# Linear attention into a mixture of experts: the route's exponential and first rows moved, sixteen key projections as two column tiles, loads and fills in smaller pieces

## The chip, the cores and the metric

The kernel runs on one core of one Trainium2 chip. The metric is device time in microseconds; 427.6 us is the median of three runs of the kernel before (426.96 to 427.92). A smaller number is better.

## What is computed

Linear attention over 4 batches, 8 heads, 576 positions and head width 64, whose output rows (2304 tokens of 512) go through a mixture of 8 experts with one expert per token and a capacity of 576 rows per expert:

```python
def phi(x):
    proj = np.einsum('bhsd,df->bhsf', x, w_phi)
    proj = proj - np.max(np.abs(proj), axis=-1, keepdims=True)
    return np.concatenate([np.exp(proj), np.exp(-proj)], axis=-1)
q_p, k_p = (phi(q), phi(k))
kv = np.einsum('bhsf,bhsd->bhfd', k_p, v)
z = np.sum(k_p, axis=2)
num = np.einsum('bhsf,bhfd->bhsd', q_p, kv)
den = np.einsum('bhsf,bhf->bhs', q_p, z)[..., None] + 1e-06
x = num / den                                  # one row of 512 per token
...
logits = x @ w_gate
expert_idx = np.argmax(logits, axis=1)         # and its softmax weight
h = np.maximum(np.einsum('ecd,edf->ecf', disp, w1), 0.0)
y = np.einsum('ecf,efd->ecd', h, w2)
out[i] = gate_w[i] * y[expert_idx[i], pos[i]]  # rows beyond capacity stay zero
```

## The kernel before

The tokens are worked in two passes `p` of 1152 rows (nine blocks `r` of 128), the heads in two groups `g` of four. Each pass has 18 key items and then 18 query items, 72 in all; the loop in `attention` goes over steps `t`, and an item's stages run at lags behind the step in which its projection is made. Items 0 to 17 are the first pass's keys, 18 to 35 its queries, 36 to 53 the second pass's keys, 54 to 71 its queries. All engines' instructions are issued in the order in which this loop writes them, so each engine's queue is an order by hand.

A key item is: `project` (lines 246 to 261), which multiplies a block of `stk` by the two halves `whi` and `wlo` of `w_phi` into `pr` in PSUM (two buffers); `center` (lines 263 to 272) on VectorE, the maximum `m` and the difference `d` (three buffers), each followed by `tick`; `k_exp` on ScalarE, two exponentials `kp` (lines 315 and 316); and four steps later `kv_sum` (line 342), the product of `kp` and the values into `acc`, written as two 64-wide halves. A query item is: projection, `d`, four transposes `pt` (line 356), two exponentials `qp`, and `q_num` (line 371), also in 64-wide halves; then `rows_out` divides.

`stk` is made from a loaded block `px` by ScalarE (line 194, a copy to f16) and GpSimd (line 195, the remainder); `x_split` issues both. The table `plan` gives the steps of each split and, eight steps ahead of it, of its load (`x_load`, line 186), on SP's queue. `beat[0]` is the last `d`; a load that is `paced` waits for it. The gate's share of the values is worked by `vgate` in units of four blocks (lines 219, 229 and 241), in the first pass at steps 2, 5, 9, 13 and 16 and the next two.

`route` works out, for a group of blocks (9, then 4, 3 and 2), which expert each token goes to and at what row of `xs`. It is a list of small steps; `tick` and the loop let one or two of them run at a time, between the attention's own VectorE operations. `sm_t` is one PSUM bank in which the small results lie. For the first group the list also finds the expert with most tokens: `swaps` (a matmul of totals, three VectorE steps, then `swap_all`, nine small GpSimd operations), which swaps the experts' places. `perm["s"]` (written as `perms` in the trace) is each expert's first row. `exps` (line 481) is the exponential `es` of the logits on ScalarE; `sums` reduces it.

```python
            *([number, exps] if late else [exps] if old is None else []),
            lambda: v.tensor_reduce(rn[:, 0], oh.rearrange("p n e -> p e n"), AX.X, ALU.add),
            run_total,
            *([*swaps(), rest, rest, rest] if old is None else []),
            lambda: v.tensor_tensor(sel, oh, perm["s"].unsqueeze(1).to_broadcast([P, n, NE]), ALU.mult),
```

Then `scatter` (line 459) writes rows to `xs` from GpSimd's queue, from step 56 on. Before that `xs` is filled with zeros by `fill_xs` from SP. After attention the experts run one after the other: `ffn1` (lines 814 to 817), `relu`, `ffn2` (lines 845 to 848) and a scatter to `out`.

## Time and profile before

| | |
|---|---|
| median of three runs | 427.6 us (426.96 to 427.92) |
| the profiled execution | 425.98 us, of which its span 424.2 us |
| PE busy | 405.1 us, 95% of the span |
| PEld (weight loads) busy | 357.7 us, 84% |
| VectorE (DVE) busy | 265.9 us, 63% |
| ScalarE (ACT) busy | 245.9 us, 58% |
| GpSimd (POOL) busy | 175.4 us, 41% |
| mean granted TensorE clock | 0.99 |

Times in rows are from the span's start. A busy share is a mean over stages with different limits, so the rows further down are taken stage by stage: which engine waits, and for what. "[2.33 <-DVE d L269]" behind an instruction says that its engine was idle for 2.33 us before it and that the instruction at line 269 released it. A matmul's record is longer than its step, since matmuls are pipelined; the distance of two starts is the step. An f32 matmul shows as two records.

### The profile page before, as it was taken

To read this page: it belongs to the slowest core of one execution; us is meant where nothing else is said; L and a number is where in the kernel's file an instruction comes from. 1 tells how busy PE (TensorE), PEld (TensorE's weight loads), DVE (VectorE), ACT (ScalarE), POOL (GpSimd) and SP (SyncE) were. 2 spreads that over 40 slices of the span, in tenths; PEclk is the share of its full clock that TensorE was granted. 3 is DMA by queue.
4 is the path that set the end of the run, shared out by engine and by line. 5 is a ranking of instruction groups with operands and counts; after the bars stand their busy time and mean duration, and the time that the engine had idled before them with its cause. 6 is when DMAs were issued, how large, how long until landed. Compare 5 with 4: busy or idle time off the path is not lost.

```text
span 424.2 us, 12166 instructions
## 1 busy us (share of the span) xinstructions
PE 405.1 (95%) x4813; PEld 357.7 (84%) x4813; DVE 265.9 (63%) x585; ACT 245.9 (58%) x452; POOL 175.4 (41%) x215
## 2 busy tenths in 40 slices
PE   6999999999799989999999999999999999999992
PEld 4788888888789878989979898989898998799871
DVE  5776898887788797833247975757475464156410
ACT  3978687779776766712146855656565454155410
POOL 1848566448576778730035306042241500160011
PEclk9999999999899999999999999999999999999997
DMA  7990599489506743479007995977959176210010
GB/s 254 388 353 5 170 328 372 138 287 307 172 6 222 227 171 107 175 249 368 5 32 223 341 338 192 331 226 224 324 179 349 64 240 228 93 36 0 2 51 29
DMA packets 42715, 82.78 MB, mean 195 GB/s; under 512 B 4351, under 2 KB 9343, under 8 KB 42624
## 3 DMA queue, kind: packets, MB, share of 16 engines
q1 hardware_dynamic: 38080, 72.13, 50.5%
q0 software_dynamic: 4544, 9.47, 6.2%
q8 instruction: 53, 0.87, 0.9%
q14 instruction: 38, 0.31, 0.2%
HBM read 62.65 MB, written 24.30 MB: 205 GB/s over the span
## 4 chain that ended last, share of the span: by engine, by line
PE 83%; POOL 4%; issue 4%; ACT 4%; DVE 3%; DMA 1%; POOLq 0%; ACTq 0%
PE ph L814 9%; PE ph L815 9%; PE ph L817 9%; PE acc L342 8%; PE acc L371 5%; PE sm L847 4%; PE sm L845 4%; PE sm L848 4%; PE ph L845 4%; PE ph L847 4%; PE ph L848 4%; PE pr L259 3%; PE pr L260 2%; PE pr L254 2%; PE pt L747 2%
## 5 line engine op out<-in xcount | busy, mean ns | idle before, releaser
L169 POOL DMA_INDIRECT out<-y,it x22 | 24.4, 1111 | 164.4 <-ACT y L860 86.7
L123 DVE TENSOR_TENSOR l<-raw,h 128x512 fp32r<-128x512 f32 x118 | 79.6, 706 | 19.6 <-ACT h L117 16.9
L195 POOL TENSOR_TENSOR stk<-px,stk 64x1024 f16<-64x1024 f32 (+1 forms) x30 | 70.8, 2363 | 38.6 <-ACT stk L194 37.7
L814 PE MATMUL ph<-xh,h 128*128 128x256 f32 (+3 forms) x292 | 79.4, 298 | 0.1
L815 PE MATMUL ph<-xh,l 128*128 128x256 f32 (+3 forms) x292 | 78.9, 296 | 0.0
L117 ACT ACTIVATE h<-raw 128x512 fp32r<-128x512 f32 x128 | 75.7, 629 | 0.0
L828 ACT ACTIVATE h<-ph 128x256 fp32r<-128x256 f32 (+3 forms) x67 | 28.8, 429 | 53.6 <-PE ph L817 52.9
L831 DVE SCALAR_TENSOR_TENSOR h<-ph,h 128x256 fp32r<-128x256 f32 (+2 forms) x91 | 33.3, 388 | 39.2 <-ACT h L828 38.8
L814 PEld LDWEIGHTS ph<-xh,h 128*128 128x128 f32 x292 | 55.6, 191 | 1.2 <-issue 0.2
L815 PEld LDWEIGHTS ph<-xh,l 128*128 128x128 f32 x292 | 55.7, 191 | 0.9
L265 DVE TENSOR_REDUCE m<-pr 128x4 f32<-128x512 f32 x72 | 49.2, 684 | 8.6 <-PE pr L260 5.1
L269 DVE TENSOR_TENSOR d<-pr,m 128x512 f32<-128x512 f32 x72 | 49.7, 691 | 4.0 <-ACT kp L316 0.4
L817 PE MATMUL ph<-xh,h 128*128 128x256 f32 (+3 forms) x292 | 50.9, 296 | 0.0
L342 PE MATMUL acc<-v,kp 128*64 128x73 f32 (+1 forms) x1280 | 46.3, 231 | 1.1 <-issue 1.1
L342 PEld LDWEIGHTS acc<-v,kp 128*64 128x64 f32 (+1 forms) x1280 | 40.7, 138 | 5.8 <-issue 2.6
L371 PE MATMUL acc<-kv,qp 128*64 128x73 f32 x1152 | 44.5, 229 | 0.0
L371 PEld LDWEIGHTS acc<-kv,qp 128*64 128x64 f32 x1152 | 39.1, 136 | 6.0 <-issue 5.7
L817 PEld LDWEIGHTS ph<-xh,h 128*128 128x128 f32 x292 | 42.7, 191 | 0.6
L259 PE MATMUL pr<-whi,stk 128*128 128x128 f16 x260 | 36.9, 223 | 2.6 <-DVE d L269 2.3
L260 PE MATMUL pr<-wlo,stk 128*128 128x128 f16 x260 | 36.4, 221 | 0.0
L194 ACT ACTIVATE stk<-px 64x1024 f16<-64x1024 f32 (+1 forms) x30 | 34.5, 1150 | 0.5
L358 ACT ACTIVATE qp<-pt 128x512 f32<-128x512 f32 x36 | 21.5, 596 | 21.1 <-PE pt L356 21.0
(163 smaller groups left out, 715.8 us busy)
## 6 DMA issues: line engine op xcount, KB each, us to landing
raw<-in_w SPq DMA_DIRECT2D x28, 1024.0 KB, 7.9
xs<-fill SPq DMA_DIRECT2D x18, 514.0 KB, 6.1
xr<-xs SPq DMA_DIRECT2D x24, 257.0 KB, 7.9
raw<-in_w SPq DMA_DIRECT2D x8, 512.0 KB, 4.3
vt<-in_vT SPq DMA_DIRECT2D x3, 1152.0 KB, 12.7
v<-in_vv SPq DMA_DIRECT2D x2, 1314.0 KB, 11.9
px<-in_kT SPq DMA_DIRECT2D x5, 512.0 KB, 8.5
px<-in_qT SPq DMA_DIRECT2D x4, 640.0 KB, 9.3
```

Of the source, the lines that this page charges most:

```text
L117: nc.scalar.activation(hi, a, AF.Copy)
L123: engine.tensor_tensor(lo, a, hi.bitcast(F32), ALU.subtract)
L195: return lambda: nc.gpsimd.tensor_tensor(t[other], x, t[own], ALU.subtract)
L259: nc.tensor.matmul(pr[:, j], lt, whi, start=True, stop=False)
L260: nc.tensor.matmul(pr[:, j], lt, wlo, start=False, stop=True)
L265: nc.vector.tensor_reduce(m.rearrange("p a b -> p (a b)"), pr, AX.X, ALU.max, apply_absolute_value=True)
L269: beat[0] = nc.vector.tensor_tensor(d, pr, m.to_broadcast([P, 4, NF]), ALU.subtract)
L342: nc.tensor.matmul(acc[f:f + D, a, j * GC:(j + 1) * GC], kp[lo:hi, j, a, f:f + D], vt[lo:hi, r, h * GC:(h + 1) * GC], start=first and j == ...
L371: nc.tensor.matmul(num[lo:hi, g, j * GC:(j + 1) * GC], qp[:, a, j, lo:hi], kv_t[b][:, a, 4 * g + j], start=(a == 0), stop=(a == 1))
L814: nc.tensor.matmul(acc, hi[:, k, fs], xh[:, k, o:o2], start=(k == 0), stop=False)
L815: nc.tensor.matmul(acc, lo[:, k, fs], xh[:, k, o:o2], start=False, stop=False)
L817: nc.tensor.matmul(acc, hi[:, k, fs], xl[:, k, o:o2], start=False, stop=(k == 3))
```

## The change

Five things are changed. `exps` of the first group goes behind `swaps`. A copy puts `perm["s"]` into the PSUM bank, and `sel` reads it there. Sixteen key projections (all of the first pass that use `stk`, eleven, and the second pass's first five) are written as two 64-wide halves for each of `whi` and `wlo`. The loads of keys and queries come in halves, a step apart, paced by the beat, seven steps ahead of the split (four for the first pass's queries); the second pass's values come in twelve pieces in place of four. The fills are 36 of 128 rows from step 19 to 53, where they were 18 of 256 rows from step 18 to 47.

```diff
--- before.py
+++ after.py
@@ -150,14 +150,8 @@
         tc.add_manual_dep(dma.ins, beat[0].ins.name, mybir.DependencyInfo(
             mybir.DependencyClass.Sync, mybir.DependencyReason.DATA), reason="pace")
 
-    def fill_xs(i, n):
-        r0, r1 = (NE * slots * j // n for j in (i, i + 1))
-        nr = (r1 - r0) // P
-        if nr:
-            paced(nc.sync.dma_start(xs[r0:r0 + nr * P, :].rearrange("(r p) c -> p r c", p=P),
-                                    fill.unsqueeze(1).to_broadcast([P, nr, XW])))
-        if r1 - r0 - nr * P:
-            nc.sync.dma_start(xs[r0 + nr * P:r1, :], fill[0:r1 - r0 - nr * P])
+    def fill_xs(r0, r1):
+        paced(nc.sync.dma_start(xs[r0:r1, :], fill[0:r1 - r0]))
 
     tokf = cpool.tile([P, NT // P], F32, tag="tokf", name="tokf")
     nc.gpsimd.iota(tokf, pattern=[[P, NT // P]], base=SKIP, channel_multiplier=1,
@@ -183,7 +177,9 @@
             raw_x[kind, p, g, c] = px_p.tile([P, 2, c1 - c0], F32, tag=f"px{c}", name="px")
         lo, hi = (0, cut) if cut > 0 else (-cut, c1 - c0)
         src = (kT if kind == "k" else qT)[2 * g:2 * g + 2, :, p * TP + c0 + lo:p * TP + c0 + hi]
-        nc.sync.dma_start(raw_x[kind, p, g, c][:, :, lo:hi], src.rearrange("i d c -> d i c"))
+        dma = nc.sync.dma_start(raw_x[kind, p, g, c][:, :, lo:hi], src.rearrange("i d c -> d i c"))
+        if beat[0] is not None:
+            paced(dma)
 
 
     def x_split(kind, p, g, c, odd):
@@ -256,8 +252,14 @@
         else:
             for j in range(4):
                 lt = stk[kind, p, g, c, j % 2][:, j // 2, cols]
-                nc.tensor.matmul(pr[:, j], lt, whi, start=True, stop=False)
-                nc.tensor.matmul(pr[:, j], lt, wlo, start=False, stop=True)
+                if kind == "q" or p and (g or r >= 5):
+                    nc.tensor.matmul(pr[:, j], lt, whi, start=True, stop=False)
+                    nc.tensor.matmul(pr[:, j], lt, wlo, start=False, stop=True)
+                    continue
+                for w in (whi, wlo):
+                    for o in range(0, P, D):
+                        nc.tensor.matmul(pr[o:o + D, j], lt[:, o:o + D], w, start=w is whi, stop=w is wlo,
+                                         skip_group_check=True)
         return pr
 
     def center(pr):
@@ -532,11 +534,12 @@
             lambda: v.scalar_tensor_tensor(ef, lt, 0.0, io, ALU.is_ge, ALU.mult),
             lambda: v.tensor_reduce(flat(ix), ef, AX.X, ALU.min),
             lambda: v.tensor_tensor(oh, ix.to_broadcast([P, n, NE]), io, ALU.is_equal),
-            *([number, exps] if late else [exps] if old is None else []),
+            *([number, exps] if late else []),
             lambda: v.tensor_reduce(rn[:, 0], oh.rearrange("p n e -> p e n"), AX.X, ALU.add),
             run_total,
-            *([*swaps(), rest, rest, rest] if old is None else []),
-            lambda: v.tensor_tensor(sel, oh, perm["s"].unsqueeze(1).to_broadcast([P, n, NE]), ALU.mult),
+            *([*swaps(), exps, rest, rest, rest, lambda: v.tensor_copy(sm_t[:, TOT:TOT + NE], perm["s"])]
+              if old is None else []),
+            lambda: v.tensor_tensor(sel, oh, sm_t[:, TOT:TOT + NE].unsqueeze(1).to_broadcast([P, n, NE]), ALU.mult),
             lambda: v.tensor_reduce(flat(sl), sel, AX.X, ALU.add),
             positions,
             *([] if late or old is None else [exps, rest, rest, rest]),
@@ -630,7 +633,9 @@
                 ends.append(max(split))
                 if x[:2] != (K, 0):
                     free = ends[-4] if len(ends) > 3 else 6
-                    load_at.setdefault(max(free + 2, min(split) - 8), []).append((*x, c))
+                    first = max(free + 2, min(split) - (4 if x[:2] == (Q, 0) else 7))
+                    for i in range(2):
+                        load_at.setdefault(first + i, []).append((*x, c, (1 - 2 * i) * (runs[c][1] - runs[c][0]) // 2))
 
         plan(0, [(5, 6), (12, 13), (15, 16), (25, 26), (31, 32), (42, 44), (46, 49)])
         plan(1, [(3, 4), (10, 11), (19, 21), (23, 24), (28, 29), (37, 39), (55, 51), (57, 53)])
@@ -662,7 +667,8 @@
             for i, f in enumerate(parts):
                 early.setdefault(t + min(i, 3 - t) if t == 2 else t + i, []).append(f)
 
-        FILLS = [*range(18, 36, 3), *range(36, 48)]
+        FILLS = [*range(19, 36, 2), *range(36, 54), *range(37, 54, 2)]
+        filled = [0]
         OPEN = 56
         depth = 4
         for t in range(len(items) + depth):
@@ -684,15 +690,13 @@
                 for _ in range(4):
                     if pending:
                         step()
-            if t in FILLS:
-                for i in range(len(FILLS)):
-                    if FILLS[i] == t:
-                        fill_xs(i, len(FILLS))
-            if t in (19, 23):
-                vt_load(1, 0, NBLK, (t - 19) // 4)
-                v_load(1, 0, NBLK, (t - 19) // 4)
+            for _ in range(FILLS.count(t)):
+                fill_xs(filled[0], min(filled[0] + P, NE * slots))
+                filled[0] += P
+            if 19 <= t < 31:
+                (vt_load if t % 2 else v_load)(1, (t - 19) // 2 % 3 * 3, (t - 19) // 2 % 3 * 3 + 3, (t - 19) // 6)
             if t == 54:
-                assert swapped
+                assert swapped and filled[0] >= NE * slots
                 for e in range(NE):
                     who[e] = nc.values_load(perm_i[0:1, e:e + 1], engines=[mybir.EngineType.SP], min_val=0,
                                             max_val=NE - 1)
```

ScalarE's order in the second pass's key phase. `kp` are a key item's exponentials, `stk` the copy of a split, `es` the route's exponential. Before:

```order
L194 ACTIVATE stk<-px 64x1280
L315 ACTIVATE kp<-d 128x4x128
L316 ACTIVATE kp<-d 128x4x128
L481 ACTIVATE es<-sm 128x72
L315 ACTIVATE kp<-d 128x4x128
L316 ACTIVATE kp<-d 128x4x128
L315 ACTIVATE kp<-d 128x4x128
L316 ACTIVATE kp<-d 128x4x128
```

Now, from the next item on:

```order
L317 ACTIVATE kp<-d 128x4x128
L318 ACTIVATE kp<-d 128x4x128
L317 ACTIVATE kp<-d 128x4x128
L318 ACTIVATE kp<-d 128x4x128
L190 ACTIVATE stk<-px 64x1280
L317 ACTIVATE kp<-d 128x4x128
L318 ACTIVATE kp<-d 128x4x128
L317 ACTIVATE kp<-d 128x4x128
L318 ACTIVATE kp<-d 128x4x128
L483 ACTIVATE es<-sm 128x72
```

`es` stood one item behind the first `stk` half; now it stands four items further down, behind the second half too.

VectorE's order in the same phase. `m` and `d` are an item's maximum and difference, `sm<-oh` the sum of the one-hot rows at old line 536 (now 538), `rb` its cast, `swap<-sm` the first step of `swaps`. Before:

```order
L269 TENSOR_TENSOR d<-pr,m 128x512
L265 TENSOR_REDUCE m<-pr 128x4
L536 TENSOR_REDUCE sm<-oh 128x8
L269 TENSOR_TENSOR d<-pr,m 128x512
L265 TENSOR_REDUCE m<-pr 128x4
L476 CAST rb<-sm 128x8
L269 TENSOR_TENSOR d<-pr,m 128x512
L265 TENSOR_REDUCE m<-pr 128x4
L269 TENSOR_TENSOR d<-pr,m 128x512
L350 COPY kv<-acc 128x2x292
L265 TENSOR_REDUCE m<-pr 128x4
L503 TENSOR_REDUCE swap<-sm 128x1
```

Now:

```order
L271 TENSOR_TENSOR d<-pr,m 128x512
L267 TENSOR_REDUCE m<-pr 128x4
L538 TENSOR_REDUCE sm<-oh 128x8
L478 CAST rb<-sm 128x8
L271 TENSOR_TENSOR d<-pr,m 128x512
L267 TENSOR_REDUCE m<-pr 128x4
L271 TENSOR_TENSOR d<-pr,m 128x512
L267 TENSOR_REDUCE m<-pr 128x4
L505 TENSOR_REDUCE swap<-sm 128x1
L271 TENSOR_TENSOR d<-pr,m 128x512
```

`rb` and the first step of `swaps` each come up by one item.

VectorE's order at the end of that phase, where `sel` is made. Before:

```order
L269 TENSOR_TENSOR d<-pr,m 128x512
L265 TENSOR_REDUCE m<-pr 128x4
L539 TENSOR_TENSOR sel<-oh,perms 128x72
L269 TENSOR_TENSOR d<-pr,m 128x512
L540 TENSOR_REDUCE sm<-sel 128x9
```

Now:

```order
L271 TENSOR_TENSOR d<-pr,m 128x512
L540 COPY sm<-perms 128x8
L267 TENSOR_REDUCE m<-pr 128x4
L542 TENSOR_TENSOR sel<-oh,sm 128x72
L271 TENSOR_TENSOR d<-pr,m 128x512
L543 TENSOR_REDUCE sm<-sel 128x9
```

The copy `sm<-perms` stands ahead of the last item's `m`, and `sel` reads `sm` in place of `perms`.

## Rows read from the trace of the kernel before

**Rows 1.** The page: PE busy in tenths, 40 slices; the chain that ended last.

```profile
PE   6999999999799989999999999999999999999992
...
PE 83%; POOL 4%; issue 4%; ACT 4%; DVE 3%; DMA 1%; POOLq 0%; ACTq 0%
```

**Rows 2.** Stretches: length; busy PE, PEld, DVE, ACT, POOL; granted clock, DMA share, GB/s.

```profile
106.00:108.40 2.40, 0.07 (x4) 0.01 (x1) 0.94 (x3) 1.43 (x4) 2.05 (x1) 1.00 1.02 377
108.40:111.70 3.30, 3.30 (x43) 2.96 (x44) 2.63 (x6) 3.04 (x5) 0.56 (x1) 0.50 0.86 279
```

**Rows 3.** Timeline of PE: start, us, engine line operation, count [idle before <-releaser].

```profile
104.82 1.25 PE L342 MATMUL acc<-v,kp 128*64 128x73 f32 x32
108.40 0.29 PE L259 MATMUL pr<-whi,stk 128*128 128x128 f16 x1 [2.33 <-DVE d L269]
...
109.36 2.21 PE L342 MATMUL acc<-v,kp 128*64 128x73 f32 x32
...
112.18 1.25 PE L342 MATMUL acc<-v,kp 128*64 128x73 f32 x32
```

**Rows 4.** Timeline of VectorE (DVE), the reduction at line 536.

```profile
107.46 0.29 DVE L536 TENSOR_REDUCE sm<-oh 128x8 f32<-128x72 bf16 x1 [3.50 <-ACT es L481]
```

**Rows 5.** Timeline of ScalarE (ACT), 103 to 109 us.

```profile
103.46 0.61 ACT L316 ACTIVATE kp<-d 128x512 f32<-128x512 f32 x1
...
105.03 1.25 ACT L194 ACTIVATE stk<-px 64x1280 f16<-64x1280 f32 x1
...
107.22 0.21 ACT L481 ACTIVATE es<-sm 128x72 f32<-128x72 f32 x1
108.45 0.63 ACT L315 ACTIVATE kp<-d 128x512 f32<-128x512 f32 x1 [1.02 <-DVE d L269]
```

**Rows 6.** Timeline of VectorE, the products named sel.

```profile
125.27 0.17 DVE L546 TENSOR_TENSOR sel<-sm,oh 128x72 f32<-128x72 f32 x1
...
149.50 3.04 DVE L539 TENSOR_TENSOR sel<-oh,perms 128x32 f32<-128x32 bf16 x1
```

**Rows 7.** Timeline of GpSimd (POOL) at the same times.

```profile
123.45 2.13 POOL L195 TENSOR_TENSOR stk<-px,stk 64x1024 f16<-64x1024 f32 x1 [1.02 <-ACT stk L194]
...
149.98 2.49 POOL L123 TENSOR_TENSOR l<-raw,h 128x512 fp32r<-128x512 f32 x2
```

**Rows 8.** Timeline of PE in the second pass's query phase.

```profile
147.64 1.24 PE L371 MATMUL acc<-kv,qp 128*64 128x73 f32 x32
...
149.80 1.24 PE L371 MATMUL acc<-kv,qp 128*64 128x73 f32 x32
152.82 0.18 PE L455 MATMUL sm<-oh,tri 128*128 128x32 bf16 x1 [1.78 <-DVE sm L540]
...
153.92 1.24 PE L371 MATMUL acc<-kv,qp 128*64 128x73 f32 x32
```

**Rows 9.** Timeline of PE in the first pass's key phase.

```profile
20.10 1.25 PE L342 MATMUL acc<-v,kp 128*64 128x73 f32 x32
21.28 0.23 PE L259 MATMUL pr<-whi,stk 128*128 128x128 f16 x1
...
21.68 0.22 PE L260 MATMUL pr<-wlo,stk 128*128 128x128 f16 x1
21.83 1.26 PE L342 MATMUL acc<-v,kp 64*64 64x73 f32 x64
```

**Rows 10.** Timeline of GpSimd, from the first to the seventh step of swap_all.

```profile
115.44 0.25 POOL L488 TENSOR_SCALAR swap<-swap 128x1 f32<-128x1 f32 x1 [0.53 <-DVE swap L505]
...
117.59 0.24 POOL L494 TENSOR_SCALAR perms<-perme 128x8 f32<-128x8 f32 x1
```

**Rows 11.** Groups by line, 12 to 125 us: busy us, mean ns | idle before.

```profile
L342 PE MATMUL acc<-v,kp 128*64 128x73 f32 x960 | 38.9, 233 | 1.1 <-issue 1.1
```

**Rows 12.** A query split on ScalarE; DMA issues of 10 to 40 us.

```profile
30.54 1.25 ACT L194 ACTIVATE stk<-px 64x1280 f16<-64x1280 f32 x1
...
px<-in_qT SPq DMA_DIRECT2D x2, 640.0 KB, 12.2
```

## The prediction

> **What bounds the kernel now.** I read the chain of waits first: 83% of the end-setting chain is TensorE's own work, 4% each ScalarE, GpSimd and "issue" [rows 1]. So the kernel is PE-bound, and a change is worth what it does to PE's order: idle time taken out, or matmul time added. Next I looked at the 40 slices of PE's busy share: nines, but for the start, the end and two slices, a 7 (106 to 117 us) and an 8 (148 to 159) [rows 1]. Each edit of the route's code touches one of the two.
>
> The first lies in the second pass's key phase. PE works for 0.07 of 2.40 us between 106.0 and 108.4, and the following 3.3 us run at a granted clock of 0.50, which is the 1.2 GHz level, where it was 1.00 until PE stood still [rows 2]. PE's own rows show why it stood: the projection at 108.40 waited 2.33 us for a `d` of VectorE [rows 3]. VectorE in turn sat 3.50 us ahead of the reduction at line 536, and that was released by ScalarE's `es`, the route's exponential [rows 4]. ScalarE was not slow with `es` itself (0.21 us); it came to it only at 107.22, because its queue held exponentials and a 1.25 us `stk` copy ahead of it [rows 5]. The `d` that PE needed stands behind line 536 in VectorE's order and needs nothing of the route.
>
> The second lies in the second pass's query phase. `sel` at line 539 took 3.04 us at 149.50 for 128x32 elements, and ended at 152.5, when GpSimd's two line-123 operations ended (149.98 + 2.49 = 152.47) [rows 6, 7]. The like operation at line 546, of the same size class but with one input in PSUM, took 0.17 us at 125.27 while GpSimd was inside a 2.13 us operation [rows 6, 7]. So what costs is not the arithmetic but two SBUF inputs beside a GpSimd operation. PE waited 1.78 us for the sum after `sel` [rows 8].
>
> **The exponential moved: -3.9 us.** `es` now stands behind `swaps`, line 536 loses its wait, and `rb` moves up a place. The key phase's pace is one projection and one key-value group in 1.73 us (20.10 to 21.83) [rows 9]. The groups at 104.82, 109.36 and 112.18 [rows 3] are 7.36 us apart for two steps, against 3.46: 3.9 us, of which 2.4 is the idle time and the rest the low clock. Whether it all comes back depends on what is late next. VectorE's next `d` reuses a buffer of three, free when the exponential pair that ends at 103.46 + 0.61 = 104.07 is done [rows 5], so it can run at 104.1 in place of 107.7. PE would project again at 104.82 + 1.18 = 106.0 and, at 1.73 us, read the pair that ends 107.2 (behind the 105.03 copy) at about 108.3. Taking ScalarE's queue forward at 1.04 us a pair and 1.2 us a copy, each later pair is done at least 0.7 us ahead of its use. I therefore take the whole 3.9. Bounds: 1.2 (the 1.02 us that ScalarE itself idles at 108.45 plus `es` [rows 5], if its queue is the limit) and 3.9.
>
> **First rows moved: -1.9 us.** A new 128x8 copy puts `perm["s"]` in PSUM, and all four `sel` read it there, so they should take the 0.17 us of line 546. PE's query groups start 2.16 us apart (147.64, 149.80), then 4.12 (153.92) [rows 8]: 1.96 us over pace, less 0.1 for the position matmuls that run in it. I take 1.9. The bounds are 1.8, PE's idle time itself, and 2.0. The new copy costs VectorE some 0.2 us, beside ScalarE's and PE's work. It is a wait too: VectorE now stands at the copy until GpSimd has written `perms`, 117.83 - 115.44 = 2.39 us after it starts [rows 10], and GpSimd starts only behind its second `stk` operation. ScalarE's queue, taken forward as above, gives up the second `stk` half at 110.5; GpSimd's 2.6 us for it and the 2.39 end at 115.5. The copy's turn comes just after PE's projection of step 53, at 106.0 + 5 x 1.73 = 114.7, so VectorE may stand there for under 1 us, with one `m` behind it that PE needs two steps later. I take 0. Below, a gain has no reason. Above, the copy could be shut out by GpSimd's next `stk` operation for 2.13 us [rows 7]; I take the near end, because the copy has one SBUF input, as line 546 has.
>
> The Trainium skill (SBUF — State Buffer, "Who interferes with whom") says that VectorE and GpSimd share a port pair as an exclusive lock, which a VectorE operation takes with two SBUF inputs against a GpSimd operation that reads SBUF, or in a two-port mode that copies may enter. By the first half the new copy is free, by the second it would wait; no row here shows a copy from SBUF to PSUM, and by the second the sum would be 2.1 us smaller at most.
>
> **Sixteen projections as two column tiles: 0.** Before, eight 128-wide matmuls, (21.68 - 21.28)/7 = 57 ns apart, 0.46 us together. Then 0.15 us to the key-value group, so 0.09 more than the 57. Ahead of a projection, the last of the 32 matmuls of the group at 20.10 starts at 20.10 + 1.25 - 0.23 = 21.12 and the projection 0.16 later, where the group's own step is 33 ns: 0.13 more [rows 9, 11]. Both gaps lie where the width changes between 128 and 64. Now there are sixteen matmuls, each 64 wide with its own weight load. The trace has no 64-wide f16 matmul. Nearest is the key-value group itself: 64-wide f32 in two column halves, 33 ns per load and matmul. Upper end: 90 ns (33 for a load plus 57 for the stream, nothing overlapped); lower end: 28 ns (57 shared by two halves). I take 33: 0.53 us a projection, +0.07, times 16 = +1.1 us. The gaps: of the eleven projections in the first pass, five lie between key-value groups and lose both (-1.1); three come after gate groups (line 219), lose the trailing one (-0.3); three come after a 128-wide transpose and swap one for the other. Of the five in the second pass two gain gaps before the 128-wide transposes of queries (+0.13, +0.22), one loses 0.09, two are even. Sum 1.1 - 1.1 - 0.3 + 0.3 = 0. Ends: -1.1 (28 ns) and +14.6 (90 ns).
>
> The Trainium skill speaks against this edit: TensorEngine Tiling, "Restrictions and Gotchas", says column tiling excludes the fast weight load, and TensorE: Matmul & The Clock Gate, "LDWEIGHTS", gives columns / 1.2 ns otherwise, 53 ns here as an estimate. If those loads ran one after another the edit would cost 5.2 us. The f32 group, 64 wide as well, keeps 33 ns in this trace.
>
> **Loads and fills: 0.** Query and key loads come in halves and wait for the beat, four to seven steps ahead of their split in place of eight. The first split of a query reads at 30.54 [rows 12]; its halves are issued at steps 8 and 9, the steps of the projections at 21.28 and, 1.73 later, 23.0 [rows 9], so the second has 7.5 us. Before, such loads landed 12.2 us after issue [rows 12], but that was at twice the size, behind the opening's other loads. I count 0, with up to 5 us for the worst case. Thirty-six fills of 128 rows replace eighteen of 256; the last goes out at step 53, three steps (over 5 us) before the first scatter, which needs them all. No wait in the two stretches above names a DMA, so the fills' going elsewhere frees nothing. 0, with the scatter's wait as the cost if they land later.
>
> **Sum.** -3.9 - 1.9 + 0 + 0 = -5.8 us. From 159 us to the last slice PE's share is all nines [rows 1], so what is gained before arrives at the end. The profiled execution took 425.98 us (span 424.2 plus 1.78 around it), so it would be 420.2. The median of the three runs shown, 427.6, is 1.6 higher; the forecast is for that: **421.8 us**.
>
> **Rivals.**
> 1. *The hole refills.* ScalarE's queue, or the copy behind GpSimd, may take over as the wait. Only 1.2 us of the first stall returns: 427.6 - 1.2 - 1.9 = 424.5. For it speaks the backlog that held `es` until 107.22, against it the 0.7 us of slack reckoned above.
> 2. *The other side: the two column halves do not overlap.* Then a load and matmul takes 57 to 90 ns. The break-even is where sixteen projections cost 5.8 + 1.1 = 6.9 us, 0.43 each, 55 ns a pair; at 57 the time is 428.0, at 90 436.4. Against it: the key-value group holds 33 ns [rows 9]. By the page's 53 ns it would be 427.0.
> 3. *Loads late.* If the halves land as late as the old loads, two or three splits come 3 to 5 us late: 425 to 431. For it only the old landing times; against it their half size and the emptier queue.
> 4. *The change misses.* `sel` keeps its stall, or line 536 another wait on ScalarE: 423.7 or 425.7.
>
> **How the numbers follow.** Forecast 0.68, rival 1 0.17, rival 2 0.06, rival 3 0.06, rival 4 0.03. A difference under 0.2% (0.9 us) cannot be told from none here. Faster: all of the forecast, rivals 1 and 4 and a third of 3, 0.90. Rivals 2 and 3 give the rest, 0.05 for the same and 0.05 for slower. The range runs from the column tiles' best end and a microsecond and a half of scatter (419.2) to a microsecond past rival 1 (425.5).
>
> **What would show it.** In the new profile the reduction at the old line 536 has no wait on ScalarE, PE has no idle stretch after its key-value group near 106 and the clock stays 1.00 there; the four `sel` take under 0.25 us and PE no longer waits for the sum after them; a 64-wide projection takes 0.45 to 0.55 us. The forecast is wrong if PE's waits in 100 to 125 us name ScalarE or GpSimd, if the pairs are over 55 ns apart, or if a `stk` copy waits for a DMA.

## The result and the profile after

The change takes 420.53 us (median of six runs, 418.88 to 422.01) against 427.28 us of the kernel before (six runs, 423.96 to 427.95): a ratio of 0.985, 95% interval 0.981 to 0.989. The forecast was 421.8 us. The profiled execution took 420.59 us (span 418.9) against 425.98 (span 424.2).

The page of the change: PE's busy share in tenths, the clock granted to it, the instruction queue of the DMA section, the chain that ended last.

```profile
PE   5999899999999999999999999999999999999992
...
PEclk9999999999999999999999999999999999999998
...
q8 instruction: 54, 0.88, 0.9%
...
PE 82%; POOL 4%; DVE 4%; issue 3%; DMA 3%; ACT 2%; POOLq 0%; SPq 0%; ACTq 0%; DVEq 0%
```

The 7 and the 8 in the middle of PE's row [rows 1] are gone, and the clock stays at its upper level until the last slice. A new 8 stands at 42 to 52 us; in it lies a wait for GpSimd that comes below.

The exponential's place. VectorE's timeline in the change, the reduction of line 536 (now 538) and the next `d`:

```profile
103.94 0.29 DVE L538 TENSOR_REDUCE sm<-oh 128x8 f32<-128x72 bf16 x1
...
104.34 0.68 DVE L271 TENSOR_TENSOR d<-pr,m 128x512 f32<-128x512 f32 x1
```

PE's timeline in the change, key-value groups (line 344 was 342), then query groups (373 was 371) and the position matmuls (457 was 455):

```profile
100.66 0.92 PE L344 MATMUL acc<-v,kp 128*64 128x73 f32 x21
102.14 0.60 PE L344 MATMUL acc<-v,kp 128*64 128x73 f32 x11 [0.55 <-issue]
...
104.95 1.25 PE L344 MATMUL acc<-v,kp 128*64 128x73 f32 x32
106.69 1.27 PE L344 MATMUL acc<-v,kp 128*64 128x73 f32 x32
108.46 1.25 PE L344 MATMUL acc<-v,kp 128*64 128x73 f32 x32
...
115.38 1.26 PE L344 MATMUL acc<-v,kp 64*64 64x73 f32 x64
...
144.17 1.24 PE L373 MATMUL acc<-kv,qp 128*64 128x73 f32 x32
...
146.34 1.24 PE L373 MATMUL acc<-kv,qp 128*64 128x73 f32 x32
147.50 0.19 PE L457 MATMUL sm<-oh,tri 128*128 128x32 bf16 x1
...
148.62 1.24 PE L373 MATMUL acc<-kv,qp 128*64 128x73 f32 x32
```

The reduction no longer waits (3.50 us in [rows 4]). The group that started at 104.82 before [rows 3] starts at 104.95; the next two follow 1.74 and 1.77 us apart, where 4.54 and 2.82 lay between them [rows 3]. The query groups that were 4.12 us apart [rows 8] are 2.28 apart, and the position matmul waits for nothing. New is the 0.55 us of "issue" within the group at 100.66; it comes back below.

The four `sel` and the copy in the change, by tile and by line: duration in ns (least, median, most), first and last start.

```profile
L542 DVE TENSOR_TENSOR sel<-oh,sm x4: 158/174/219, 116.1 to 166.6; 128x72 f32<-128x72 bf16 x1, 128x32 f32<-128x32 bf16 x1, 128x24 f32<-128x24 bf16 x1, 128x16 f32<-128x16 bf16 x1
...
L540 DVE COPY sm<-perms x1: 170/170/170, 115.3 to 115.3; 128x8 f32<-128x8 f32 x1
```

The 3.04 us of [rows 6] are 0.22 at most, though the first `sel` (116.09) runs while GpSimd is inside its `stk` operations (115.58 to 119.82).

The column tiles. PE's timeline in the change, first pass (x2 is a pair of halves; both start within the same row):

```profile
24.07 0.62 PE L215 MATMUL pt<-vt,gwp 128*32 128x128 f32 x11
25.30 0.42 PE L215 MATMUL pt<-vt,gwp 128*32 128x128 f32 x5 [0.60 <-issue]
...
27.97 1.20 PE L344 MATMUL acc<-v,kp 128*64 128x73 f32 x32
29.01 0.22 PE L261 MATMUL pr<-whi,stk 128*64 128x128 f16 x2
29.06 0.22 PE L261 MATMUL pr<-wlo,stk 128*64 128x128 f16 x2
...
29.45 1.20 PE L344 MATMUL acc<-v,kp 128*64 128x73 f32 x32
...
43.27 0.23 PE L256 MATMUL pr<-whi,stk 128*128 128x128 f16 x1 [1.05 <-POOL stk L191]
```

A projection takes 29.45 - 29.01 = 0.44 us for sixteen matmuls, 28 ns each, and the gaps to the key-value groups are gone: 1.48 us an item against 1.73 [rows 9]. Yet PE then waits 1.05 us for GpSimd's part of a query's `stk`, and 0.60 us for "issue".

So each term seemed to have come out about as forecast. The experiments show that two of the four, the tiles and the loads, had not.

### The profile page after: what moved, and what is told of

Its sections match the earlier page's. It is cut to its first block, busy times and chain, and to the rows that moved or that the text cites. A ratio compares the mean times of both kernels' runs of the same rounds, so it can differ in the third digit from the quotient of the medians.

```text
span 418.9 us, 12495 instructions
## 1 busy us (share of the span) xinstructions
PE 402.6 (96%) x4941; PEld 356.0 (85%) x4941; DVE 263.2 (63%) x586; ACT 245.2 (59%) x452; POOL 175.6 (42%) x215
## 4 chain that ended last, share of the span: by engine, by line
PE 82%; POOL 4%; DVE 4%; issue 3%; DMA 3%; ACT 2%; POOLq 0%; SPq 0%; ACTq 0%; DVEq 0%
PE ph L818 9%; PE ph L819 9%; PE ph L821 9%; PE acc L344 7%; PE acc L373 5%; PE sm L851 4%; PE sm L849 4%; PE sm L852 4%; PE ph L849 4%; PE ph L851 4%; PE ph L852 4%; PE pr L256 2%; POOL stk L191 2%; PE pt L358 2%; PE pt L751 2%
## 5 line engine op out<-in xcount | busy, mean ns | idle before, releaser
L344 PE MATMUL acc<-v,kp 128*64 128x73 f32 (+1 forms) x1280 | 44.9, 228 | 0.6 <-issue 0.6
L849 PE MATMUL sm<-h,h 128*128 128x512 f32 x72 | 29.0, 403 | 0.1
L256 PE MATMUL pr<-whi,stk 128*128 128x128 f16 x196 | 27.7, 221 | 1.5 <-POOL stk L191 1.4
```

What stands on the lines that cost most here:

```text
L256: nc.tensor.matmul(pr[:, j], lt, whi, start=True, stop=False)
L344: nc.tensor.matmul(acc[f:f + D, a, j * GC:(j + 1) * GC], kp[lo:hi, j, a, f:f + D], vt[lo:hi, r, h * GC:(h + 1) * GC], start=first and j == ...
L849: nc.tensor.matmul(py[0:m], h_t[f][:, s0:s0 + m], hi, start=(f == 0), stop=False, skip_group_check=True)
```

## Experiments

Three groups of four kernels (the `e` runs but for e4_no_tiles, the `f` runs with e4_no_tiles, the `g` runs), each group on one chip, beside its own runs of the kernel before (medians 427.11, 426.25 and 426.56 us). Ratios are to those. A ratio's interval is some 0.2 to 0.4% wide to either side.

| kernel | exponential | first rows | tiles | q and k loads | fills, values | us | ratio (95%) |
|---|---|---|---|---|---|---|---|
| the change | yes | yes | yes | halves | small | 420.53 | 0.985 (0.981 to 0.989) |
| e1_exp | yes | - | - | whole | old | 425.41 | 0.995 (0.993 to 0.997) |
| e2_sel | - | yes | - | whole | old | 431.87 | 1.014 (1.009 to 1.018) |
| e3_tiles | - | - | yes | whole | old | 429.51 | 1.005 (1.002 to 1.007) |
| e7_old_loads | yes | yes | yes | whole | old | 426.29 | 0.999 (0.997 to 1.001) |
| f1_loads_only | - | - | - | halves | small | 423.86 | 0.995 (0.993 to 0.998) |
| f2_whole_loads | yes | yes | yes | whole | small | 423.60 | 0.994 (0.992 to 0.996) |
| f3_old_fills_values | yes | yes | yes | halves | old | 428.95 | 1.007 (1.004 to 1.010) |
| e4_no_tiles | yes | yes | - | halves | small | 419.75 | 0.986 (0.982 to 0.989) |
| g1_exp_sel | yes | yes | - | whole | old | 421.08 | 0.987 (0.983 to 0.990) |
| g2_early_split | yes | yes | yes | halves | small | 420.84 | 0.986 (0.983 to 0.990) |
| g3_combo | yes | yes | 11 | halves | respread | 421.56 | 0.988 (0.984 to 0.992) |
| g4_no_tiles_fills | yes | yes | - | halves | respread | 419.42 | 0.983 (0.979 to 0.986) |

### One part at a time

The edits are parts of the change, each made on the kernel before.

**e1_exp**, the exponential alone:

```diff
-            *([number, exps] if late else [exps] if old is None else []),
+            *([number, exps] if late else []),
-            *([*swaps(), rest, rest, rest] if old is None else []),
+            *([*swaps(), exps, rest, rest, rest] if old is None else []),
```

> The kernel before with one edit: the route's exponential behind the swaps. Theory (the terms add): the reduction behind it loses its 3.50 us wait, PE's idle 2.33 us at 108 us and the 1.2 GHz level after it go, the groups of items 43 to 49 take 10.4 us in place of 14.3, and the time falls by 3.9 us, to about 0.991 of before. Rival 1 (ScalarE's queue or another wait takes over): only 1.2 us, 0.997. Rival 2 (the gain needs the faster column tiles ahead of it): under 1 us.

Measured: 0.995, 1.7 us by the medians. The hole is gone, as the theory says (the reduction runs at 103.49, with no wait), but 0.79 us of "issue" came into a key-value group (at 108.15), and the query phase lost some 2.5 us in a way not seen before: from the last key-value product to the experts' first it took 39.4 us, against 36.9 in the change, where `sel` is as short. ScalarE's timeline of e1_exp there:

```profile
135.22 0.60 ACT L358 ACTIVATE qp<-pt 128x512 f32<-128x512 f32 x1 [2.49 <-PE pt L356]
```

PE had finished those transposes at 133.7 (they start at 133.10), 1.5 us earlier. Three more such late starts, 0.3 to 1.0 us each, follow at 140, 145 and 149 us. All four kernels of this group show such starts, none of the other eight and neither of the first two profiles; the four ran on one chip. So all four ratios of this group may hold a cost that is not the edits'. It was not tried on a second chip, and stays open.

**e2_sel**, the first rows alone:

```diff
-            *([*swaps(), rest, rest, rest] if old is None else []),
-            lambda: v.tensor_tensor(sel, oh, perm["s"].unsqueeze(1).to_broadcast([P, n, NE]), ALU.mult),
+            *([*swaps(), rest, rest, rest, lambda: v.tensor_copy(sm_t[:, TOT:TOT + NE], perm["s"])]
+              if old is None else []),
+            lambda: v.tensor_tensor(sel, oh, sm_t[:, TOT:TOT + NE].unsqueeze(1).to_broadcast([P, n, NE]), ALU.mult),
```

> The kernel before with one edit: the copy of the first rows into PSUM, and sel reading it there. Theory: sel falls from 3.04 us to about 0.2, PE's wait of 1.78 us before the position sum goes, and the time falls by 1.8 to 1.9 us (0.9956). Rival 1 (the copy itself, with both its ends on ports that GpSimd holds, now waits): the copy takes over 1 us, some of the gain is lost, above 0.998. Rival 2 (the wait only moves on to the next sum): no gain, 1.000.

Measured: 1.014, 4.8 us slower by the medians, which no theory had. The four `sel` are short, and PE's query groups come 1.8 us closer, as forecast. Then VectorE's timeline of e2_sel shows, a few steps later:

```profile
155.07 5.30 DVE L550 TENSOR_SCALAR drop<-pr 128x4 f32<-128x4 f32 x1
```

GpSimd's timeline of the same kernel at that time:

```profile
154.40 2.52 POOL L123 TENSOR_TENSOR l<-raw,h 128x512 fp32r<-128x512 f32 x2
156.86 1.04 POOL L412 TENSOR_TENSOR xr<-nb,rd 128x512 f32<-128x512 f32 x1
157.86 2.47 POOL L123 TENSOR_TENSOR l<-raw,h 128x512 fp32r<-128x512 f32 x2
```

And PE's, with a granted clock of 0.50 (the 1.2 GHz level) from 161.9 to 165.3 behind its wait:

```profile
161.01 0.22 PE L259 MATMUL pr<-whi,stk 128*128 128x128 f16 x1 [3.62 <-DVE d L269]
```

An operation on 128x4 elements, 0.16 us in the kernel before (between two operations of GpSimd), stood until GpSimd's whole run of five operations was through: 155.07 + 5.30 = 160.37, and 157.86 + 2.47 = 160.33. It has one SBUF input, and writes to SBUF. The Trainium skill (SBUF — State Buffer, "Who interferes with whom") has a rule for it: a VectorE operation in a two-port mode is shut out as well as one with two SBUF inputs. This row agrees; whether `drop` runs in that mode, no view shows.

The new copy, from SBUF to PSUM, is not shut out. In f3_old_fills_values, a later run with the same two edits of the route, it falls inside a `stk` operation of GpSimd. VectorE's and GpSimd's timelines of that run:

```profile
122.53 0.16 DVE L546 COPY sm<-perms 128x8 f32<-128x8 f32 x1
...
121.64 2.14 POOL L197 TENSOR_TENSOR stk<-px,stk 64x1024 f16<-64x1024 f32 x1
```

So the expectation's first rival falls: the copy takes 0.16 us there. The exponential's hole is still in e2_sel, and it cost less than before. PE's timeline of e2_sel:

```profile
104.27 1.25 PE L342 MATMUL acc<-v,kp 128*64 128x73 f32 x32
107.85 0.23 PE L259 MATMUL pr<-whi,stk 128*128 128x128 f16 x1 [2.32 <-DVE d L269]
...
108.40 1.25 PE L342 MATMUL acc<-v,kp 128*64 128x73 f32 x32
110.13 1.25 PE L342 MATMUL acc<-v,kp 128*64 128x73 f32 x32
```

PE stood 2.32 us, as before (2.33), but here the granted clock stayed at 1.00 from 106 to 112 us, where before it fell to 0.50 [rows 2]. The two steps took 5.86 us, against 7.36 [rows 3].

**e3_tiles**, the sixteen projections alone (the hunk on `project`):

> The kernel before with one edit: sixteen key projections as two column tiles. Theory: the first pass's key items come 0.25 us sooner where they stand between key-value groups (1.9 us over items 7 to 17), of which about 1.05 us goes back in a wait for GpSimd's stk of a query at 43 us and 0.3 at the start of the second pass: 0.5 to 0.9 us less (0.998 to 0.9988). Rival 1 (nothing is given back that would not be idle anyway): 1.9 us, 0.9955. Rival 2 (the tiles only shift the wait for stk): no change, 1.000.

**e7_old_loads**, the change with loads, values and fills as before:

> The change without its part on loads and fills (exponential, first rows and column tiles as changed; loads, values and fills as before). Theory (loads and fills cost nothing): the same as the change within noise, 0.985 to 0.987. Rival (the smaller pieces are what lets the rest arrive): more than 1 us slower than the change, 0.988 or more, with a wait for px or xs in the chain. Second rival (the smaller pieces cost something, such as PE's 0.55 us issue gap at 102 us): 0.983.

Measured: 1.005 and 0.999. For e3_tiles theory and rivals all fall: the tiles alone cost 2.4 us by the medians. Part of that may be the open cost of this group, but 1.7 us lie in the first pass, ahead of all late starts (table below). For e7_old_loads the first rival holds, though its wait is of another kind than it said. PE's timeline of e7_old_loads:

```profile
24.22 0.62 PE L219 MATMUL pt<-vt,gwp 128*32 128x128 f32 x11
26.82 0.42 PE L219 MATMUL pt<-vt,gwp 128*32 128x128 f32 x5 [1.98 <-issue]
```

PE stops inside a group of sixteen matmuls of one kind, and waits for no engine. There are three more such stops, 1.67 us at 33.13, 1.07 at 78.36 and 0.39 at 111.27. What arrives just before each is a packet of 16 KB on the queue that the page calls instruction. The DMA view of e7_old_loads from 20.0 to 24.3 us has no such packet, with the engines full (share above 100%):

```profile
q1 hardware_dynamic: 1043, 1.65, 106.0%
```

and from 24.39 to 24.45 us it has one:

```profile
q8 instruction: 1, 0.02, 114.0%
```

Its time is 1.14 x 0.06 us x 16 = 1.09 us, so it ends at 25.5, and PE goes on 1.3 us later. In the change the like packet starts between 22.79 and 22.85, ends at 23.9, and PE goes on at 25.30, 1.4 us later. Over all fourteen profiles, every "issue" stop of PE of 0.3 us or more in the first 130 us, 28 in all, ends 1.3 to 1.6 us behind the end of such a packet.

Where the 28 stops lie is the stronger sign. Count all of TensorE's instructions in a trace, matmuls, weight loads and semaphore instructions, ahead of the first one behind a stop: 706 and 962 before, 706 and 4290 in the change, 706, 961, 3009 and 4545 in e7_old_loads. In all 28 it is 706 plus a multiple of 256, to within one, whatever the kernel. (Each kernel of the first group has one more stop, of 0.34 to 0.41 us, among its late starts; it lies at no such count, and over 4 us behind a packet.) 16 KB over 256 are 64 bytes an instruction; and the 128 matmuls that the tiles add, with their 128 weight loads, add one packet: 53 before, 54 in the change. (g3_combo has 56; nothing here says why.) So these packets bring TensorE its instructions, 256 at a time, and a stop is a block that came late. The two stops of the kernel before, in PE's timeline, are of this kind:

```profile
27.11 0.92 PE L342 MATMUL acc<-v,kp 128*64 128x73 f32 x21 [0.64 <-issue]
...
33.36 0.73 PE L342 MATMUL acc<-v,kp 128*64 128x73 f32 x15 [0.43 <-issue]
```

### Which loads, and do the tiles pay at all

The edit of f2_whole_loads, on the change:

```diff
-                    first = max(free + 2, min(split) - (4 if x[:2] == (Q, 0) else 7))
-                    for i in range(2):
...
+                    load_at.setdefault(max(free + 2, min(split) - 8), []).append((*x, c))
...
-        if beat[0] is not None:
-            paced(dma)
```

**f1_loads_only**:

> The kernel before with the loads and fills of the change alone (halves and pace for keys and queries, values in twelve pieces, 36 fills of 128 rows); exponential, first rows and projections as before. Theory F (the 16 KB blocks of TensorE's instructions come over the same DMA engines, and large loads make them late): the two issue gaps of before at 27 and 33 us (0.64 and 0.43 us) shrink, no new ones come, and the time falls by 1 to 2 us, ratio 0.995 to 0.998; the 2.33 us hole at 108 us and the 1.78 us at 152 us stay. Theory of the prediction (loads and fills are worth nothing by themselves): 1.000.

**f2_whole_loads**:

> The change, but with the key and query loads whole, unpaced and eight steps ahead, as before; fills and values in the change's small pieces. Theory F1 (these loads are what makes the instruction blocks late): issue gaps of over 1 us come back near 25, 32 or 78 us, and the ratio to before is 0.994 to 0.998, near the run that kept all loads and fills as before. Theory F2 (values and fills do it): no such gaps, 0.985 to 0.988, as the change.

**f3_old_fills_values** (the other half of the loads' hunk undone):

> The change, but with the values' four large loads and the eighteen fills of before; key and query loads in paced halves. Theory F1 (key and query loads make the instruction blocks late): 0.985 to 0.988, with no issue gap over 1 us. Theory F2 (the 1152 KB values and 514 KB fills do it): gaps of over 1 us near 78 us, where the fetch came late in the run with all loads as before, and 0.992 to 0.998.

**e4_no_tiles**:

> The change without column tiles (all projections 128 wide). Theory (the tiles are worth 1.9 us in the first pass, of which 1.05 goes back in the wait for GpSimd's stk and 0.3 in the second pass): 0.5 to 0.9 us slower than the change, 0.9865 to 0.988 of before. Rival (their 128 more matmuls and loads only make the instruction blocks late): faster than the change, 0.980 to 0.984, with the issue gaps at 25 and 102 us gone.

Measured: 0.995, 0.994, 1.007 and 0.986. The first pass tells the kernels apart best, because nothing of the route's edits lies in it. Its length from the first key-value product to the first query product (13.16 to 49.12 us before), with PE's two "issue" stops near 27 and 33 us and the start of the packet ahead of the first:

| projections | q and k loads | kernels | length, us | stops, us | packet at, us |
|---|---|---|---|---|---|
| 128 wide | whole | before, e1, e2, g1 | 35.7 to 36.0 | 0.64 to 0.92; 0.43 or less | 24.2 to 24.8 |
| column tiles | whole | e3, e7, f2 | 37.7 | 1.86 to 1.98; 1.67 | 23.7 to 24.5 |
| 128 wide | halves | f1, e4, g4 | 34.6 | none | 23.1 to 23.5 |
| column tiles | halves | the change, f3 | 35.3, 34.6 | 0.60 or none | 22.8 to 23.0 |

F1 holds for these stops: the key and query loads decide. The stretch of 23 to 24 us in the kernel before and in f1_loads_only (length; busy PE, PEld, DVE, ACT, POOL; granted clock, DMA share, GB/s):

```profile
23.00:24.00 1.00, 1.00 (x27) 0.88 (x22) 1.00 (x2) 0.70 (x2) 0.00 (x0) 1.00 1.07 403
...
23.00:24.00 1.00, 1.00 (x25) 0.90 (x26) 1.00 (x2) 0.70 (x3) 0.00 (x0) 1.00 0.88 220
```

With whole loads the share is 1.05 to 1.12 in all seven kernels, with halves 0.31 to 0.98. Counted from the first key-value product, the packet starts at 11.4 to 11.6 us with whole loads and at 8.6 to 10.5 with halves. (g2 and g3, with a split a step earlier, are left out of the table: 34.2 and 34.0 us, no stops.) The tiles use up instructions faster (a projection has twice as many in the same time), so the same packet is missed by 1.9 us in place of 0.6 to 0.9. In f2_whole_loads the first pass is 2.3 us longer than in the change, of 3.1 us between the two profiled executions. The halves also go out later (the first pass's first two queries' at 21.6 and 23.0 us, where whole ones went from 13.7 on); which of the two counts, size or time, no run separates.

f3_old_fills_values fell out otherwise than both theories had it. Up to the first query product it is as short (34.6 us), but then PE stands. PE's timeline of it:

```profile
61.78 1.12 PE L364 MATMUL pt<-ident,d 128*128 128x128 f32 x4 [4.18 <-ACT qp L367]
```

ScalarE's timeline, behind which that `qp` stood:

```profile
59.72 1.06 ACT L196 ACTIVATE stk<-px 64x1024 f16<-64x1024 f32 x1 [4.80 <-issue]
```

DMA issues of f3_old_fills_values from 44 to 62 us, KB each and median us to landing:

```profile
v<-in_vv SPq DMA_DIRECT2D x2, 1314.0 KB
vt<-in_vT SPq DMA_DIRECT2D x2, 1152.0 KB, 9.0
...
px<-in_kT SPq DMA_DIRECT2D x2, 256.0 KB, 8.1
```

The halves of the first pass's queries are asked for four steps ahead in place of eight. Those of the last split go out at steps 19 and 20, and the values' first large loads at step 19 as well: the second half is issued at 51.1 us and lands at 59.6 (46.1 and 51.8 in the change). The split that needs it holds up ScalarE's queue, and behind PE's stop the granted clock is 0.50 from 61.8 to 65.2 us. Two instruction stops, 1.01 us at 108.7 and 0.47 at 114.9, come on top, and the time is some 9 us worse than the change. That is the prediction's third rival, with its price; halves of keys and queries need values in pieces.

e4_no_tiles (the reverse of e3_tiles' hunk) is as fast as the change, 0.986 against 0.985, between theory and rival: the tiles are worth nothing that can be measured here. f1_loads_only, with neither of the route's edits, is 2.4 us faster than before by the medians. Of the 2.3 us between the two profiled executions, 1.4 lie in the first pass. Another 1.2 lie in the second pass's key phase. There a new instruction stop of 1.00 us, at 101.8, which theory F had not, brings PE later to the hole; the hole is 1.05 us long in place of 2.33, and the clock stays at 1.00. What is gained there is the low clock, and the exponential's edit gains that too. In f1_loads_only the old `sel` still stalls, and now in two places (VectorE's timeline):

```profile
116.87 1.63 DVE L535 TENSOR_TENSOR sel<-oh,perms 128x72 f32<-128x72 bf16 x1
...
146.85 3.04 DVE L535 TENSOR_TENSOR sel<-oh,perms 128x32 f32<-128x32 bf16 x1
```

In e1_exp the same `sel`, unchanged, took 0.22 us at most. It depends on when it comes up beside GpSimd's operations. The second one (128x32) fell into the same operation of GpSimd, a scatter, in both kernels: 0.55 us after that began in f1_loads_only, and it stood until the two of line 123 behind it were through (149.84); 0.09 us after in e1_exp, where it took 0.18 us.

### The prediction's sum, and can it be beaten

**g1_exp_sel**, the two edits of the route together, all else as before:

> The kernel before with the two edits of the route together (exponential behind the swaps, first rows from PSUM); 128-wide projections, loads and fills as before. The prediction's sum rests on these two alone: 3.9 + 1.9 = 5.8 us, 0.986. Theory F (the route's edits give their 5 to 6 us where VectorE's order lines up with GpSimd's, and the column tiles cost 2.5 to 3.5 us when the loads are large, because TensorE's instruction blocks then come late): 0.986 to 0.989, issue gaps of 0.64 and 0.43 us at 27 and 33 us as in before, and none above 1 us. Rival (the route's edits alone are worth only what the run with tiles and old loads gave): 0.996 to 0.999, through a VectorE operation shut out by GpSimd or PE's signals late in the query phase.

Measured: 0.987, 5.5 us: the prediction's two terms, alone, give most of the 6.8 us, and the rest is within the intervals. The four `sel` take 219 ns at most. `drop` takes 0.68 us: it is shut out here too, but it comes up at 152.64, when the run of GpSimd has only until 153.30 to go.

The edits, on the change:

```diff
-        plan(0, [(5, 6), (12, 13), (15, 16), (25, 26), (31, 32), (42, 44), (46, 49)])
+        plan(0, [(5, 6), (12, 13), (14, 15), (25, 26), (31, 32), (42, 44), (46, 49)])
...
-        FILLS = [*range(19, 36, 2), *range(36, 54), *range(37, 54, 2)]
+        FILLS = [*range(19, 31, 2), *range(31, 54), *range(32, 46, 2)]
```

g2_early_split has the first, g3_combo both and tiles in the first pass alone, g4_no_tiles_fills the second and no tiles.

> The change with one entry of the split table a step earlier: the first pass's second query group at steps 14 and 15 (was 15 and 16). Theory (the column tiles' gain in the first pass goes back in PE's 1.05 us wait for GpSimd's stk at 43 us): that wait is gone, the first pass's first query product comes about 1 us sooner (47.0 us), and the time falls by up to 1 us, 0.983. Rival (the wait only moves to the next stk or to a key's d): as the change, 0.985.

> The change with column tiles in the first pass alone, the early split, and the fills spread otherwise (one a step from 31 to 53, the rest from 19 on; fewer between 95 and 115 us, more between 75 and 90). Theory F: PE's issue gap at 102 us (0.55 us, 0.83 us of time) goes since the instruction block comes sooner, the second pass loses nothing to width changes (0.36 us), and the wait at 43 us is gone: 2 us less than the change, 0.980 to 0.982. Rival (each is refilled by another wait): 0.985.

> The change without column tiles and with the fills spread as in the run before this one. Theory F: as the run without tiles (0.9857), less 0.6 to 0.8 us if the block at 99 us comes sooner: 0.984. Rival (fills do not touch the fetch): an issue gap of 0.4 us or more stays near 101 us, 0.9857; or the fills between 75 and 90 us make another fetch late there, above 0.986.

g2_early_split: the wait at 43 us shrank to 0.72 us, and the first pass took 34.2 us in place of 35.3. But in this execution the opening loads landed later (first key-value product at 13.94 in place of 12.75), and the time shows no gain (0.986). g3_combo's opening was later still, 14.5 us (0.988). Neither beats the change. g4_no_tiles_fills: PE's timeline keeps its stop,

```profile
101.90 0.60 PE L338 MATMUL acc<-v,kp 128*64 128x73 f32 x11 [0.74 <-issue]
```

so the fills' places are not what makes the block at 99 us late, and that theory falls. Its 419.42 us is the lowest median of all, but its interval overlaps that of the change and of e4_no_tiles; a version that certainly beats the change was not found.

## Why the prediction was right, and where it was not

**Exponential, -3.9: right.** In the change items 43 to 49 (104.95 to 115.38) take 10.43 us; before, 104.82 to 119.12, 14.30: -3.87. The whole of it came back, as chosen, and not the lower bound of 1.2. But 1.5 us of it is the low clock, and that is no fixed part of the hole: in e2_sel the same hole left the clock at 1.00 and cost 2.4 us. Set against such an execution the term would be 2.4.

**First rows, -1.9: right.** The shift of the query groups goes from 147.64 - 144.17 = 3.47 to 153.92 - 148.62 = 5.30: -1.83. But the reason given for the copy ("one SBUF input, as line 546 has") is not enough: `drop` in e2_sel has one SBUF input too and stood 5.30 us. The copy and the new `sel` have an end in PSUM, which `drop` and the old `sel` have not; but a reciprocal from SBUF to SBUF, `rd`, took 0.17 us at 153.68 in e2_sel, inside an operation of GpSimd (153.40 to 154.46), so that is not the whole rule. In the change itself the copy met only two small casts of GpSimd (115.18 to 115.49); in f3_old_fills_values it took 0.16 us inside a `stk` operation, so the near end was rightly taken.

**Column tiles, 0: right as a net figure, but by luck.** A matmul took 28 ns, the lower end, not the 33 chosen, and the gaps vanished as reckoned: the pace was 1.48 us. By the prediction's own sum that is -1.1 us, and e4_no_tiles shows no such gain. But of the 1.93 us that PE was ahead of before at 33 us (33.22 against 35.15), e4_no_tiles has 1.72 without them: that was the loads'. What was left out: twice the instructions (their block came 0.60 us late even with small loads, and 1.9 with the old ones), and GpSimd's `stk`, to which 1.05 us went. The second rival, halves that do not overlap, did not occur. The Trainium skill (TensorEngine Tiling (Array Packing), "Restrictions and Gotchas") says that column tiling excludes the fast weight load. The estimate made from it, loads of 53 ns one after another, did not come out: 28 ns a matmul leaves no room for that. The two halves start together, 56 ns behind the pair before, so whether their loads are fast ones these rows do not tell.

**Loads and fills, 0: this step failed.** It read the waits for data and found none in the two stretches, and counted the rest as free. On the chip they are worth 2.4 us by themselves (f1_loads_only; 1.4 of it in the first pass), and without their first half the change is 3.6 us slower (ratios 0.994 and 0.985). The time that it had at nothing is TensorE's wait for its own instructions. The sign stood in the prediction's own rows: line 342 sits idle for 1.1 us before "issue" [rows 11], which is the two stops of 0.64 and 0.43 us. The 4% "issue" of the chain [rows 1], some 15 us, is for the most part something else, and the change keeps 3% of it.

**The sum, -5.8: right.** g1_exp_sel shows the two large terms alone at -5.5 us, and the change at -6.8, with intervals of some 1.6 us to either side. Its two small terms, tiles and loads, each differ from 0 alone (+2.4, with the open cost of its group, and -2.4 us). Together, on top of the other two, they make the -1.3 us between the two kernels, which the intervals do not tell from 0. That the errors cancel was luck.

**The terms do not add one by one.** e1_exp and e2_sel alone give -1.7 and +4.8 us, together -5.5. What is shown is that `drop` met GpSimd's run at its start in e2_sel (5.30 us) and near its end in g1_exp_sel (0.68). Both single runs also carry the open late starts of their group, some 2.5 us in e1_exp, and whether these put `drop` where it fell is not shown. The first rival, "the hole refills", is what e2_sel did, by another wait and at a price the prediction had not: worse than before.

## What to carry to other kernels

When a PE-bound kernel stops inside a group of like matmuls and the profile says "issue", look for an instruction packet that landed a good microsecond earlier, and at the loads that fill the DMA engines ahead of it: here smaller and later loads moved it up, and an edit that doubled the matmuls moved the need for it up too. Whether the stops lie a fixed number of instructions apart tells such a block from other causes. A small VectorE operation beside a GpSimd chain cost 0.2 to 5.3 us here, by its kind and by where it fell, so an edit that removes one such stall must be judged with the ones behind it, and the parts of a change, tried one at a time, need not add up to it.

## What the runs showed of the hardware

TensorE's instructions came 256 at a time, in 16 KB packets of about 1.1 us, and PE stopped for up to 1.98 us when one was late behind large loads. The Trainium skill (Runtime: NRT & Kernel Launch, "Instruction fetch mechanics") describes the 16 KiB blocks and calls the cost of crossing into the next mostly hidden; here it is hidden at most crossings, not at all of them: the first 130 us have 22 packets and two stops of 0.3 us or more in the change, 21 packets and four stops in e7_old_loads.

Two column halves of 64 start together: sixteen f16 matmuls in 0.44 us, the time of eight of 128, with a gap of at most 0.1 us to a group of 64 columns beside them.

Beside GpSimd's operations, a VectorE product with two SBUF inputs (`sel`, 3.04 us) and a tensor_scalar from SBUF to SBUF (`drop`, 5.30 us, over five operations) stood until these were through; a copy from SBUF to PSUM, a product with one input in PSUM and a reciprocal from SBUF to SBUF did not (0.16, 0.22 and 0.17 us).

The late starts behind PE in the first group (up to 1.5 us after the matmul that released them) have no cause that these runs show.
